# The last expert step's second layer in two column halves, each with a bank and a store of its own

## The chip, the core and the metric

The kernel runs on one core of one Trainium2 chip. The metric is device time in microseconds of one execution. Five engines run side by side, each with its own instruction stream: PE (TensorE, matrix products; its weight loads are listed as PEld), ACT (ScalarE), DVE (VectorE), POOL (GpSimd) and SP (SyncE, which here issues the loads). They wait for each other by semaphores. PE writes into PSUM banks, from which ACT or DVE carries results to SBUF. Data go to and from HBM by DMA; the stores of this kernel's result are indirect DMAs (each row to its own place) that POOL issues.

## The reference

The first part is attention with random features over 8 batches, 8 heads and 576 positions; its result, 4608 rows (tokens) of 512, is the input `x` of a mixture of 8 experts, of which each row takes one:

```python
logits = xn @ en.T / tau
expert_idx = np.argmax(logits, axis=1)
...
gate_w = probs[np.arange(N), expert_idx]
out = np.zeros((N, D), dtype=np.float32)
for e in range(E):
    mask = expert_idx == e
    ...
    h = np.maximum(x[mask] @ w1[e], 0.0)
    out[mask] = gate_w[mask, None] * (h @ w2[e])
```

N is 4608, D (`DM` in the kernel) 512, E 8, and the hidden width F 1024.

## The kernel before

The attention part writes its rows, sorted by expert, into a table `xs` in HBM. With a row stand its router logits and, in its last element, the token's number, that is, the row of the output it belongs to. The expert part then goes through **steps** of 128 rows that all belong to one expert. Which expert and which rows a step has is only known at run time and stands in a small table `tabi`, from which the engines read registers. Steps 0 to 37 (`NSTAT` is 38) are written out in the program; `ends` is 37, the last of them. A loop at the end of the program takes further steps if the table has more; how many steps there are is copied to `nsteps` (L1318), every engine reads it (L1321), and branches (L1322). In the profiled execution the loop isn't entered.

A step's work: the first layer (rows times `w1`, the products in tiles named `pb` in the trace), the transposition of the hidden rows, and the second layer (`down`, hidden rows times `w2`, into a PSUM tile `po`). Operands are float32 split in a high and a low part (`hh`, `hl` for the hidden rows; `w2h`, `w2l` for the weights), and each product is the sum of three matmuls: high with high, high with low, low with high. `products` (L275 on) writes them out: for the second layer 8 blocks of the hidden width times 3, so 24 matmuls with 512 columns each. Since the buffer half that holds a step's weights is a register's value, the weights' address is made by a register instruction of PE's sequencer before each of these matmuls (`ISA` in the listings of order, `FUSED_REGOPS` in the trace).

`finished(v)` takes the second layer's result: it is scaled by the rows' gates into a tile `xgp` (two buffers, taken in turn), and the returned function calls `store` (L314), an indirect DMA from POOL that writes 128 rows of 512 floats to the places that the tokens' numbers in `tail` name. For the last step, `finished(ends, True)` scales columns 0 to 255 on ACT (L1158) and columns 256 to 511 on DVE (L1159), both from the one bank. One store follows, and then the copy of the step count.

The order on every engine is the order in which the program is written (`manual_schedule`). Two places matter here. Before the last step's scaling POOL has an explicit `nc.gpsimd.drain()` (L1316), behind the store of step 36. And the end of the program, behind the loop, has all engines meet; SP waits there for the semaphores of all DMAs, the stores' among them.

The end of the expert part before, L1309 to L1318:

```python
inverted(totals[batch(ends)[0]])
split("w2", ends - 1)
finished(ends - 2)()
down(ends, both)
finished(ends - 1)()
split("w2", ends)
nc.gpsimd.drain()
finished(ends, True)()
nc.gpsimd.tensor_copy(nsteps, tabi[:, 0:1])
```

Of the kernel before, what the change touches and what calls it, by code (L numbers as in the profile page):

```python
# [13 lines left out]
I32 = mybir.dt.int32  # L14
BF16 = mybir.dt.bfloat16
U16 = mybir.dt.uint16
AF = mybir.ActivationFunctionType
ALU = mybir.AluOpType
# [4 lines left out]
P = 128  # L23
B, H, S, D, M = 8, 8, 576, 64, 128
E, F = 8, 1024
N = B * S
DM = H * D
# [12 lines left out]
NPRE = 2  # L40
# [24 lines left out]
def attention_moe(ctx: ExitStack, tc: tile.TileContext, qT, kT, v1, omT, emb, tau, w1q, w2q, xs, out):  # L65
    nc = tc.nc
# [10 lines left out]
    nu = [nuu[:, a] for a in range(2)]  # L77
# [47 lines left out]
    xgp = [const.tile([P, PAY], F32, name=f"xgp{t}") for t in range(NPRE + 1)]  # L125
# [43 lines left out]
    def reg(kind, t):  # L169
        i, eng, mx = kinds[kind]  # L170
        g = t // 16
        if (kind, g) not in regs:
            n = min(16, NSTAT - g * 16)
            regs[kind, g] = nc.values_load_multi_w_load_instructions(
                tabi[i : i + 1, g * 16 : g * 16 + n], engines=[eng], min_val=0, max_val=mx,
                skip_runtime_bounds_check_because=WHY,
            )[1]
        return regs[kind, g][t % 16]
# [36 lines left out]
    def computed(wn, t, ms):  # L215
        for m in ms:
            seq[m] = len(seq)
        for o in range(NSTAT):
            apart(wn, spl.get((wn, o), ()), o, ms, t)
        if t >= NQ and (wn, t) not in mmi:  # L220
            for w in spl[wn, t - 1]:
                tc.add_manual_dep(ms[0].ins, w.ins.name, sync, reason="the weights")
        mmi.setdefault((wn, t), []).extend(ms)
# [48 lines left out]
        else:  # L272
            low()

    def products(dst, a, wn, par, cs, half, begin, end):  # L275
        ah, al = a
        _, wh, wl = W[wn]
        done = []
        for i, c in enumerate(cs):
            for k, (x, w) in enumerate(((ah, wh), (ah, wl), (al, wh))):  # L280
                if wn == "w1":
                    ws = w[:, ds(par, 1), c, half * 512 : (half + 1) * 512]
                else:
                    ws = w[:, ds(par, 1), c // 2, (c % 2) * 512 : (c % 2 + 1) * 512]
                done.append(nc.tensor.matmul(  # L285
                    dst, x[:, c * P : (c + 1) * P], ws.rearrange("p o f -> p (o f)"),
                    start=(begin and i == 0 and k == 0), stop=(end and i == len(cs) - 1 and k == 2),
                ))
        return done

    def scaled(po, xg, gate):
        nc.vector.tensor_scalar(xg[:, 0:DM], po, gate, None, op0=ALU.mult)
# [18 lines left out]
    def few(name, t, n):  # L311
        return gp.tile([P, n], F32, name=f"{name}{t}", tag=name, bufs=2)

    def store(t, xg, tail=None):  # L314
        w = nc.gpsimd.indirect_dma_start(  # L315
            out=out, out_offset=bass.IndirectOffsetOnAxis(ap=(xg[:, DM:] if tail is None else tail)[:, E : E + 1].bitcast(I32), axis=0),
            in_=xg[:, 0:DM], in_offset=None, bounds_check=N - 1, oob_is_err=False,
        )
        for o in outs:
            tc.declare_no_dep(w.ins, o.ins.name, reason="other tokens")  # L320
        outs.append(w)

    with ExitStack() as c1:
        p1 = c1.enter_context(tc.tile_pool(name="p1", bufs=2))
# [415 lines left out]
        early, spare, mid, ends, behind = {}, {}, {}, {}, []  # L740
        uses = iter(range(NTILE * 4))
        ring = lambda: next(uses) % 3
        at = lambda d, *key: d.setdefault(key, [])
# [16 lines left out]
        for i in range(NTILE + LAG + 2):  # L760
# [177 lines left out]
            if i in LOADS:  # L938
                n = LOADS[i]
# [16 lines left out]
        t = lambda n, w=E, dt=F32: once.tile([P, w], dt, name=n)  # L956
# [24 lines left out]
        cs, nt = cs_nt[:, 0, :], cs_nt[:, 1, :]  # L981
# [30 lines left out]
        both = once.tile([P, 3, E], F32, name="both")  # L1012
# [33 lines left out]
    p2 = ctx.enter_context(tc.tile_pool(name="p2", bufs=2))  # L1046
# [6 lines left out]
    def bank(name, tag, bufs=1):  # L1053
        return shared(tag) if bufs == 2 else ps.tile([P, 512], F32, name=name, tag=tag)
# [33 lines left out]
    xg, xt, hid, raws, po = {}, {}, {}, {}, {}  # L1088
# [31 lines left out]
    with tc.manual_schedule(engines={ET.PE, ET.Activation, ET.DVE, ET.Pool, ET.SP}):  # L1120
        xt[NPRE] = pre_x[0]
        turn, ends = {}, NSTAT - 1
# [28 lines left out]

        n2s, rough, nrms, totals, gates, tails = {}, {}, {}, {}, {}, {}

        def finished(v, halves=False):
            y = xgp[v % NPRE]
            if halves:
                p, m = po.pop(v), DM // 2
                nc.scalar.activation(y[:, 0:m], p[:, 0:m], AF.Copy, scale=gates[v])  # L1158
                nc.vector.tensor_scalar(y[:, m:DM], p[:, m:DM], gates[v], None, op0=ALU.mult)  # L1159
            else:  # L1160
                scaled(po.pop(v), y, gates[v])
            return lambda: store(v, y, tails[v])
        batch = lambda t: divmod(t - NPRE, 3)

# [29 lines left out]
        def down(u, cs):  # L1194
            if cs[0] == 0:
                po[u] = bank(f"po{u}", f"kv{u % 2}")
            par = reg("par", u) if u >= NQ else 0
            computed("w2", u, products(po[u], hid[u], "w2", par, cs, 0, cs[0] == 0, cs[-1] == 7))
# [5 lines left out]
        low, high, both = range(4), range(4, 8), range(8)  # L1204
        for t in range(NPRE, NSTAT):
# [11 lines left out]
            if early:  # L1217
                wn = joined(t - 1)
# [91 lines left out]
        inverted(totals[batch(ends)[0]])  # L1310
        split("w2", ends - 1)
        finished(ends - 2)()
        down(ends, both)
        finished(ends - 1)()
        split("w2", ends)
        nc.gpsimd.drain()  # L1316
        finished(ends, True)()
        nc.gpsimd.tensor_copy(nsteps, tabi[:, 0:1])  # L1318


    tot = nc.values_load(nsteps[4:5, 0:1], min_val=0, max_val=NSTEP, skip_runtime_bounds_check_because=WHY)  # L1321
# [70 lines left out]
```

## Time and profile before

| | us |
|---|---|
| median of 3 timed runs | 632.24 (632.17 to 633.24) |
| the profiled execution's own time | 632.94 |
| its span, first to last instruction of the program | 631.3 |
| PE busy | 620.7 (98%) |
| POOL busy | 421.7 (67%) |

The span is 1.6 us shorter than that execution's time; what lies around it is not in the trace. The granted clock of PE is 0.999 of full speed over the span. PE is busy nearly throughout, but its last matmul ends at about 625.4, and the last 5.9 us of the span belong to what comes behind it: scaling, store, the step count, and the meeting of the engines at the end. The rows for that stretch stand in the section behind the next one. In the profile "busy" leaves out register, branch and semaphore instructions; their groups are found by asking for a source line.

### The profile page before, as it was taken

To read this page: it belongs to the slowest core of one execution; us is meant where nothing else is said; L and a number is where in the kernel's file an instruction comes from. 1 tells how busy PE (TensorE), PEld (TensorE's weight loads), DVE (VectorE), ACT (ScalarE), POOL (GpSimd) and SP (SyncE) were. 2 spreads that over 40 slices of the span, in tenths; PEclk is the share of its full clock that TensorE was granted. 3 is DMA by queue.
4 is the path that set the end of the run, shared out by engine and by line. 5 is a ranking of instruction groups with operands and counts; after the bars stand their busy time and mean duration, and the time that the engine had idled before them with its cause. 6 is when DMAs were issued, how large, how long until landed. Compare 5 with 4: busy or idle time off the path is not lost.

```text
span 631.3 us, 19167 instructions
## 1 busy us (share of the span) xinstructions
PE 620.7 (98%) x6337; PEld 531.3 (84%) x6338; DVE 493.2 (78%) x916; ACT 432.9 (69%) x1136; POOL 421.7 (67%) x603
## 2 busy tenths in 40 slices
PE   9999999999999999999999999999999999999996
PEld 8999999998978788888888888888888888888884
DVE  5799899898889836779787877778687886878754
ACT  6999899899997327676756666656666656675640
POOL 3013344356787544588897878787887989797952
PEclk9999999999999999999999999999999999999999
DMA  7655776777772488698887796968687786878541
GB/s 258 217 153 168 225 200 210 220 221 251 245 256 87 153 271 265 199 258 231 246 204 245 177 263 189 229 203 229 208 212 239 202 247 175 246 202 236 172 117 46
DMA packets 143262, 132.18 MB, mean 209 GB/s; under 512 B 107766, under 2 KB 107894, under 8 KB 143168
## 3 DMA queue, kind: packets, MB, share of 16 engines
q1 hardware_dynamic: 136544, 109.96, 61.3%
q0 software_dynamic: 6480, 20.91, 8.6%
q8 instruction: 57, 0.93, 0.6%
q14 instruction: 37, 0.30, 0.2%
q10 hardware_dynamic: 144, 0.07, 0.0%
HBM read 83.78 MB, written 21.97 MB: 168 GB/s over the span
## 4 chain that ended last, share of the span: by engine, by line
PE 70%; DVE 3%; ACT 2%; issue 0%; POOL 0%; ACTq 0%; DVEq 0%
PE pb L285 31%; PE po L285 31%; PE fs_o L285 2%; PE pb L374 1%; PE nuu L483 1%; ACT ftq L388 1%; PE pb L267 1%; PE fs_a L285 1%; DVE nmq L378 1%; PE kva L406 1%; PE pb L463 0%; DVE qp L470 0%; DVE xr L508 0%; ACT qp L468 0%; ACT sq L296 0%
## 5 line engine op out<-in xcount | busy, mean ns | idle before, releaser
L240 POOL TENSOR_TENSOR w2l<-raww,w2h 128x256 f32 x128 | 142.8, 1116 | 7.6
L240 POOL TENSOR_TENSOR w1l<-raww,w1h 128x256 f32 (+1 forms) x130 | 114.0, 877 | 14.5 <-DVE w1h L234 6.0
L285 PE MATMUL po<-w2h,hh 128*128 (+1 forms) x288 | 112.2, 390 | 0.0
L285 PE MATMUL po<-w2h,hl 128*128 (+1 forms) x288 | 112.1, 389 | 0.0
L285 PE MATMUL po<-w2l,hh 128*128 (+1 forms) x288 | 112.0, 389 | 0.0
L285 PE MATMUL pb<-w1h,xh 128*128 (+1 forms) x280 | 109.3, 390 | 0.0
L285 PE MATMUL pb<-w1h,xl 128*128 (+1 forms) x280 | 109.0, 389 | 0.0
L285 PE MATMUL pb<-w1l,xh 128*128 (+1 forms) x280 | 108.9, 389 | 0.0
L1110 DVE COPY pl<-pb 128x512 uint16<-128x512 uint16 x68 | 46.8, 690 | 59.9 <-ACT pl L1106 59.3
L1106 ACT ACTIVATE pl<-pb 128x512 uint16<-128x512 uint16 x68 | 39.5, 584 | 71.8 <-PE pb L285 69.4
L388 ACT ACTIVATE ftq<-pb,nmq 128x128 f32<-128x128 f32 x288 | 80.0, 413 | 3.6 <-DVE nmq L378 3.6
L315 POOL DMA_INDIRECT y<-xgp,tail x36 | 44.8, 1246 | 53.8 <-DVE w1h L234 27.8
L388 ACT ACTIVATE ftk<-pb,nmk 128x128 f32<-128x128 f32 x272 | 75.9, 470 | 4.9 <-DVE nmk L378 4.9
L1128 DVE COPY wd<-t 128x1024 uint16<-128x1024 uint16 x68 | 64.2, 945 | 1.5 <-DMA t<-pl 1.5
L1144 ACT ACTIVATE hh<-wd 128x1024 fp32r<-128x1024 f32 x34 | 36.2, 1063 | 41.3 <-DVE wd L1128 36.7
L285 PEld LDWEIGHTS po<-w2h,hh 128*128 128x128 f32 x288 | 54.1, 188 | 11.2
L285 PEld LDWEIGHTS po<-w2l,hh 128*128 128x128 f32 x288 | 54.1, 188 | 11.2
L285 PEld LDWEIGHTS po<-w2h,hl 128*128 128x128 f32 x288 | 54.0, 187 | 11.2
L285 PEld LDWEIGHTS pb<-w1h,xl 128*128 128x128 f32 x280 | 52.6, 188 | 10.9
L285 PEld LDWEIGHTS pb<-w1l,xh 128*128 128x128 f32 x280 | 52.6, 188 | 11.0
L285 PEld LDWEIGHTS pb<-w1h,xh 128*128 128x128 f32 x280 | 52.5, 187 | 10.7
L582 POOL DMA_INDIRECT xs<-xr,posi x36 | 36.4, 1011 | 36.8 <-PE nuu L463 26.4
(346 smaller groups left out, 1265.7 us busy)
## 6 DMA issues: line engine op xcount, KB each, us to landing
raww<-w1q SPq DMA_DIRECT2D x38, 512.0 KB, 4.0
raww<-w2q SPq DMA_DIRECT2D x38, 512.0 KB, 5.2
qt<-qT SPq DMA_DIRECT2D x36, 256.0 KB, 3.7
kt<-kT SPq DMA_DIRECT2D x35, 256.0 KB, 3.4
xg<-xs SPq DMA_DIRECT2D x23, 260.5 KB, 3.0
xgp<-xs SPq DMA_DIRECT2D x15, 260.5 KB, 4.9
rf<-w1q SPq DMA_DIRECT2D x4, 512.0 KB
rf<-w2q SPq DMA_DIRECT2D x4, 512.0 KB, 5.8
```

The source lines that it names most:

```text
L240: ils.append(eng.tensor_tensor(at(l, d)[:, c], raw[:, c], at(h, d)[:, c].bitcast(F32), op=ALU.subtract))
L267: nc.tensor.transpose(bank[:, c * P : (c + 1) * P], src[:, o + c * P : o + (c + 1) * P], ident)
L285: done.append(nc.tensor.matmul(dst, x[:, c * P : (c + 1) * P], ws.rearrange("p o f -> p (o f)"), start=(begin and i == 0 and k == 0), stop ...
L315: w = nc.gpsimd.indirect_dma_start(out=out, out_offset=bass.IndirectOffsetOnAxis(ap=(xg[:, DM:] if tail is None else tail)[:, E : E + 1].b ...
L374: nc.tensor.matmul(st["pj" + w, i, a][:, c, :], st[w, i][r, c, :], om[r, :], start=True, stop=True)
L378: nc.vector.tensor_reduce(nm, st["pj" + which, i, a], axis=AX.X, op=ALU.max, negate=True)
L388: nc.scalar.activation(ft[:, h, :], pj[:, h, :], AF.Exp, bias=nm[:, h : h + 1])
L582: w = nc.gpsimd.indirect_dma_start(out=xs, out_offset=bass.IndirectOffsetOnAxis(ap=posi[:, j : j + 1], axis=0), in_=xr, in_offset=None, bo ...
L1106: nc.scalar.activation(planes[1][:, o : o + 512], halved(src)[:, :, 1], AF.Copy)
L1110: nc.vector.tensor_copy(planes[0][:, o : o + 512], halved(src)[:, :, 0])
L1128: nc.vector.tensor_copy(to, src)
L1144: nc.scalar.activation(hh, wd[:, 0:F], AF.Relu)
```

## The change

The second layer of step 37 is no longer one group of 24 matmuls with 512 columns. It is two groups of 24 matmuls with 256 columns: the first writes columns 0 to 255 into the bank `po`, the second writes columns 256 to 511 into another bank (`nu[1]`, free at that time). ACT scales the first half as soon as the first group is done, and a store of its own writes it; DVE scales the second half from the other bank, and a second store writes that. For the stores the output is seen as 9216 rows of 256 floats, and the places are twice the token's number plus 0 or 1; two small DVE instructions compute them into a new tile `places`. The copy of the step count stands between the two stores.

```diff
-    def products(dst, a, wn, par, cs, half, begin, end):
+    def products(dst, a, wn, par, cs, half, begin, end, cols=slice(0, DM)):
...
-                    ws = w[:, ds(par, 1), c // 2, (c % 2) * 512 : (c % 2 + 1) * 512]
+                    ws = w[:, ds(par, 1), c // 2, (c % 2) * 512 + cols.start : (c % 2) * 512 + cols.stop]
...
-    def store(t, xg, tail=None):
+    def store(t, xg, tail=None, to=None):
+        if to is None:
+            to, at, n, cols = out, (xg[:, DM:] if tail is None else tail)[:, E : E + 1].bitcast(I32), N, slice(0, DM)
+        else:
+            to, at, n, cols = out.rearrange("n (a d) -> (n a) d", a=2), *to
         w = nc.gpsimd.indirect_dma_start(
-            out=out, out_offset=bass.IndirectOffsetOnAxis(ap=(xg[:, DM:] if tail is None else tail)[:, E : E + 1].bitcast(I32), axis=0),
-            in_=xg[:, 0:DM], in_offset=None, bounds_check=N - 1, oob_is_err=False,
+            out=to, out_offset=bass.IndirectOffsetOnAxis(ap=at, axis=0),
+            in_=xg[:, cols], in_offset=None, bounds_check=n - 1, oob_is_err=False,
         )
...
-        down(ends, both)
+        y, m, par = xgp[ends % NPRE], DM // 2, reg("par", ends)
+        places = p2.tile([P, 2], I32, name="places", bufs=1)
+        for a in range(2):
+            nc.vector.tensor_scalar(places[:, a : a + 1], tails[ends][:, E : E + 1].bitcast(I32), 2.0, float(a), op0=ALU.mult, op1=ALU.add)
+        parts = [(bank(f"po{ends}", f"kv{ends % 2}")[:, 0:m], slice(0, m)), (nu[1][:, 0:m], slice(m, DM))]
+        for p, cols in parts:
+            computed("w2", ends, products(p, hid[ends], "w2", par, both, 0, True, True, cols))
         finished(ends - 1)()
         split("w2", ends)
         nc.gpsimd.drain()
-        finished(ends, True)()
+        (p0, c0), (p1, c1) = parts
+        nc.scalar.activation(y[:, c0], p0, AF.Copy, scale=gates[ends])
+        store(ends, y, to=(places[:, 0:1], 2 * N, c0))
         nc.gpsimd.tensor_copy(nsteps, tabi[:, 0:1])
+        nc.vector.tensor_scalar(y[:, c1], p1, gates[ends], None, op0=ALU.mult)
+        store(ends, y, to=(places[:, 1:2], 2 * N, c1))
```

The old `halves` form of `finished` goes with it. What this does to the order is seen best on two engines. (`DMA` is an indirect store; `y` is the output, `xgp` the scaled rows, `tail` the token numbers.)

POOL at the end of the program, before; the rows between the two pieces belong to the loop, which isn't entered (the branch goes from the first L1322 row to the second):

```order
L240 TENSOR_TENSOR w1l<-raww_37_9042,w1h 128x1024 [waits DMAHW5_49,DVE_49]
L315 DMA y<-xgp_140,tail_8833 4608x512 [waits DMASW6_49,DVE_49,Activation_49]
L315 DMA y<-xgp_139,tail_8942 4608x512 [waits DMASW7_49,DVE_49,Activation_49]
L315 DMA y<-xgp_140,tail_9040 4608x512 [waits DMASW0_49,DVE_49]
L1318 COPY nsteps<-tabi 5x1
L1321 TENSOR_LOAD nsteps [waits Pool_49]
L1322 COMPARE_AND_BRANCH
...
L1322 ISA [waits Pool_49,Pool_sequencer_49,DMASW1_49]
L1322 UNCONDITIONAL_BRANCH
L1388 ISA [waits barrier_Pool_Activation_PE_DVE_SP_gather]
```

POOL at the same place, after:

```order
L240 TENSOR_TENSOR w1l<-raww_37_9042,w1h 128x1024 [waits DMAHW5_49,DVE_49]
L319 DMA y<-xgp_140,tail_8833 4608x512 [waits DMASW6_49,DVE_49,Activation_49]
L319 DMA y<-xgp_139,tail_8942 4608x512 [waits DMASW7_49,DVE_49,Activation_49]
L319 DMA y<-xgp_140,places 9216x256 [waits DMASW0_49,Activation_49]
L1325 COPY nsteps<-tabi 5x1
L1330 TENSOR_LOAD nsteps [waits Pool_49]
L1331 COMPARE_AND_BRANCH
...
L1331 ISA [waits Pool_49,Pool_sequencer_49,DMASW1_49]
L1331 UNCONDITIONAL_BRANCH
L319 DMA y<-xgp_140,places 9216x256 [waits DMASW2_49,DVE_49]
L1397 UNCONDITIONAL_BRANCH
```

The second store stands not only behind the copy of the step count but behind the read of it and the branch. The drain (L1316 before) stands in both ahead of the third `DMA`; this listing leaves drains out.

DVE at the end of the program, before (`po_9192`, `po_9233` and `po_9266` are the second layers of steps 35, 36 and 37):

```order
L292 TENSOR_SCALAR xgp_140<-po_9192,totalb_9145 128x512 [waits DMASW4_49]
L292 TENSOR_SCALAR xgp_139<-po_9233,totalb_9145 128x512 [waits DMASW5_49,PE_49]
L234 ISA
L234 COPY w2h<-raww_37_9217 128x1024 [waits DMAHW2_49]
L240 ISA
L240 TENSOR_TENSOR w2l<-raww_37_9217,w2h 128x1024 [waits DVE_49]
L1159 TENSOR_SCALAR xgp_140<-po_9266,totalb_9145 128x256 [waits DMASW6_49,Activation_49]
```

DVE at the same place, after:

```order
L292 TENSOR_SCALAR xgp_140<-po_9192,totalb_9145 128x512 [waits DMASW4_49]
L1315 TENSOR_SCALAR places<-tail_9040 128x1 x2
L292 TENSOR_SCALAR xgp_139<-po_9233,totalb_9145 128x512 [waits DMASW5_49,PE_49]
L234 ISA
L234 COPY w2h<-raww_37_9217 128x1024 [waits DMAHW2_49]
L240 ISA
L240 TENSOR_TENSOR w2l<-raww_37_9217,w2h 128x1024 [waits DVE_49]
L1326 TENSOR_SCALAR xgp_140<-nuu,totalb_9145 128x256 [waits DMASW6_49,PE_49]
```

The two instructions for `places` come in ahead of step 36's scaling, and the last scaling waits for PE where it waited for ACT.

## Rows read from the trace of the kernel before

**Rows 1.** The page's head, and the tail of the chain that ended last (start us, us, what).

```profile
span 631.3 us, 19167 instructions
PE 620.7 (98%) x6337; PEld 531.3 (84%) x6338; DVE 493.2 (78%) x916; ACT 432.9 (69%) x1136; POOL 421.7 (67%) x603
...
614.47 10.91 PE po L285 x48
625.38 0.03 ACTq L1158
625.40 0.05 issue
625.45 0.48 ACT xgp L1158
625.93 0.03 issue
625.96 0.49 DVE xgp L1159
626.45 0.27 issue
626.72 0.98 POOL y L315
627.70 0.16 POOL nsteps L1318
```

**Rows 2.** What SP's queue waited for, 620 to 632 us (total us, times, longest).

```profile
SPq L1321 <- POOL nsteps L1318: 16.6, 1, 16.6
SPq L1388 <- DMA y<-xgp,tail: 0.2, 1, 0.2
```

**Rows 3.** POOL's timeline to the end (start us, us, instruction [idle before <- releaser]).

```profile
619.75 0.99 POOL L315 DMA_INDIRECT y<-xgp,tail  x1 [6.46 <-DVE xgp L292]
621.50 1.92 POOL L315 DMA_INDIRECT y<-xgp,tail  x1 [0.76 <-issue]
626.72 0.98 POOL L315 DMA_INDIRECT y<-xgp,tail  x1 [3.30 <-DVE xgp L1159]
627.68 0.18 POOL L1318 COPY nsteps<-tabi 5x1 int32<-5x1 int32 x1
```

**Rows 4.** Lines L1316, and L315 at 616 to 628 us (ns min/median/max, first and last start).

```profile
L1316 POOLq DRAIN  x1: 3875/3875/3875, 621.3 to 621.3; - x1
...
L315 POOLq MOVE  x3: 29/29/29, 616.8 to 625.2; - x3
L315 POOLq EVENT_SEMAPHORE  x3: 17/1158/2094, 616.9 to 625.3; - x3
...
DMA to landing us min/median/max: 2.7/2.7/3.5
```

**Rows 5.** Lines L1322 and L1388, POOL's sequencer at the branch and the program's end.

```profile
L1322 POOLq INC_SWDGE_SEM  x1: 203/203/203, 628.7 to 628.7; - x1
...
L1388 POOLq DRAIN  x3: 109/193/585, 628.9 to 630.9; - x3
```

**Rows 6.** DVE's timeline at 615.5 to 632 us.

```profile
615.90 0.16 DVE L308 TENSOR_SCALAR totalb<-totalb 128x3 f32<-128x3 f32 x1
...
618.22 0.74 DVE L292 TENSOR_SCALAR xgp<-po,totalb 128x512 f32<-128x512 f32 x1
619.96 0.75 DVE L292 TENSOR_SCALAR xgp<-po,totalb 128x512 f32<-128x512 f32 x1 [0.99 <-PE po L285]
...
625.96 0.48 DVE L1159 TENSOR_SCALAR xgp<-po,totalb 128x256 f32<-128x256 f32 x1 [3.39 <-ACT xgp L1158]
```

**Rows 7.** PE's timeline: transposes, and step 37's first and last second-layer matmuls.

```profile
613.43 1.03 PE L267 MATMUL pb<-ident,wd 128*128 128x128 f32 x8
...
619.76 0.39 PE L285 MATMUL po<-w2h,hh 128*128 x1
619.99 0.39 PE L285 MATMUL po<-w2l,hh 128*128 x1
...
624.98 0.39 PE L285 MATMUL po<-w2h,hl 128*128 x1
```

**Rows 8.** Line L285 from 618.5 us on, PE's sequencer and weight loads.

```profile
L285 PEldq FUSED_REGOPS  x23: 46/55/60, 619.1 to 622.1; - x23
...
L285 PEld LDWEIGHTS po<-w2l,hh x10: 187/188/188, 618.4 to 624.5; 128*128 128x128 f32 x10
```

**Rows 9.** DMA from 626 to 632 us in 40 slices: busy tenths, rate, and the store's landing.

```profile
DMA  0000000000000009998300620000000000000100
GB/s 0 0 0 0 0 0 0 0 0 0 0 0 0 0 0 410 382 410 314 137 0 0 164 55 0 0 0 0 0 0 0 0 0 0 0 0 0 55 0 0
...
y<-xgp,tail POOLq DMA_INDIRECT x1, 2.7
```

More of the change, by code (lines that the diff above doesn't have):

```diff
@@ L1152, in attention_moe, with finished @@
         n2s, rough, nrms, totals, gates, tails = {}, {}, {}, {}, {}, {}
-        def finished(v, halves=False):
+        def finished(v):
             y = xgp[v % NPRE]
[L1156 to L1161, printed above, removed]
+            scaled(po.pop(v), y, gates[v])
             return lambda: store(v, y, tails[v])
```

## The prediction

> **What bounds the kernel now.** I read the chain of waits from its end. PE leads it until the last matmul ends at 625.38, and the change touches nothing ahead of step 37, so the question is what follows: ACT's half of the scaling, then DVE's half behind it, POOL's store at 626.72, the copy of the step count [rows 1]. The chain as printed ends with the copy, but the span goes on to 631.3, and the copy isn't what it waits for. SP's waits tell what is: at the end of the program SP waited 0.2 us for the landing of the last store [rows 2], that is, SP had come round from the copy and the branch and still found the store in flight. The store takes 2.7 us from issue to landing [rows 9], so it lands at 626.72 + 2.67 = 629.4, and 1.9 us more go by until the span ends. So the end is set by **the start of the last store**, and the copy comes only some 0.2 us behind it. This is the quantity to follow: in the kernel before it is 626.72.
>
> Two things hold a store back: its data and POOL. Before, it was the data: DVE ended at 625.96 + 0.48 = 626.44 and the store started 0.28 later [rows 6, 3]. POOL was ready, but not by much. Its drain (L1316) began at 621.3 and took 3.9 us, so it ended at about 625.15; it had to sit out the store of step 36, which started at 621.50, took 1.92 [rows 3] and lands 3.5 after its start, at 625.0 (it is the largest of the three landings there) [rows 4]. POOL's last register and semaphore instructions of L315 come right behind, at 625.2 and 625.3 [rows 4]. Before, this left POOL 1.1 us of slack against 626.44. The drain is in no chain of waits, since it waits in the shadow of PE.
>
> **The change part by part.** *The first half on ACT, and its store.* The first 24 matmuls end at about half of step 37, near 623, and ACT's scaling takes 0.48 [rows 1], so the data are ready before 624. But the store stands behind the same drain, and nothing that the drain waits for moves: step 36's scaling and store stay where they were. So the first store can't be issued before 625.3. How long is it from there? Three stores show two prices. The last one stood ready and started 0.28 after its data [rows 3, 6]. The stores at 619.75 and 621.50 had to be let through by a separate semaphore instruction ahead of them; they started 0.79 after DVE's ends at 618.96 and 620.71 [rows 6, 3], with the instruction's own idle time of 0.76 put down to issue. The first half's store is of the second kind (its semaphores have long been there when the drain ends, and dispatch begins then), so I take 0.75 after the semaphore instruction at 625.3: start 626.05, with 0.28 as the other bound. It is busy 0.98, as the last one was [rows 3].
>
> *The copy, its read and the branch between the stores.* By the listing of POOL's order, what stands between the stores is not the copy alone but also the read of the count and the branch of the not-entered loop. Before, the copy started 0.96 after its store's start [rows 3], and from the copy's start to the drain at the program's end it was 628.9 - 627.68 = 1.2 us, with the last instruction of the branch at 628.7 [rows 3, 5]. So after: copy at 627.0, branch done at 628.2. This stretch is covered by nothing, since POOL does it itself, between two stores.
>
> *The second store.* Its register and semaphore instructions cost 0.1 us (625.2 and 625.3 in rows 4), and dispatch 0.75 again: it starts at about **629.05**, against 626.72. Its data are there long before: see next. That is **+2.33 us** on the quantity that sets the end.
>
> *The second half on DVE.* DVE no longer waits for ACT, which takes the 0.51 us between the two halves' starts off the data's path [rows 1]. But the data's path isn't the late one any more, so it is worth nothing here.
>
> *The matmuls.* 48 with 256 columns in place of 24 with 512. Before, one starts every 0.227 us (619.76 to 624.98 in 23 steps) [rows 7]. No row shows 256 columns in this form. From below, half of that is 0.113: no cost. The nearest row is the sequencer's: it makes an address for each matmul, and between 619.1 and 622.1 it issued 23 of them, one in 0.136 us [rows 8], while PE lagged behind; with twice as many matmuls half as long this becomes the pace. 48 x 0.136 = 6.5 from 619.13, so the last matmul starts near 625.5 and ends near 625.9, 0.5 later than before; DVE is done at 626.45. The store's data are then 2.6 us early, and this cost is hidden. From above: the shown 0.188 of a weight load [rows 8] can't be the pace, since transposes with loads go by at 0.109 each ((1.03 - 0.27)/7, with 0.27 for the last one's own length) [rows 7]; if a load lay wholly bare beside each matmul, 0.109 + 0.113 = 0.222. POOL needs the data by 628.75, which holds up to a pace of 0.17 us. TensorE: Matmul & The Clock Gate of the Trainium skill, section "LDWEIGHTS (loading the stationary operand)", gives a load of 128 columns as 107 ns; by it a pair would be 107 + 109 = 216 ns if bare, a result like that upper end, and hidden if the load runs under 256 columns as it does here under 512.
>
> *Two small DVE instructions.* 0.16 each, as the small one at 615.90; they fall where DVE waits 0.99 us for PE ahead of step 36's scaling [rows 6]. Cost nothing; without that cover 0.3 us on step 36's store, and so on the drain.
>
> *The landing.* Half the bytes. The transfer itself shows as 0.8 us of busy DMA slices (some 5.5 of 0.15 us) out of the 2.67 [rows 9]; halved, it is 0.4 less: 2.3. The bounds are 2.27 and 2.67 (the upper one if half the bytes take as long); I take 2.32, **-0.35 us**. DMA: Bandwidth & Descriptors of the Trainium skill, section "Anatomy of one DMA — SWDGE (gpsimd) path", fits 2.0 us plus bytes at 436 GB/s, which is 2.6 for this store and would be 2.3 for half of it; it also has the fixed part constant, whatever the size.
>
> *After the landing.* The same 1.9 us: the engines' meeting. SP and the others now come to it early, since the count is copied 0.7 us earlier, and wait.
>
> *The sum.* +2.33 - 0.35 = **+2.0 us**. Against the profiled execution's own time of 632.94 this is 634.9; that execution is 0.7 above the median of the timed runs, 632.24, so for the median I say **634.2**. With the bounds (dispatch 0.28 twice: -0.9; landing 2.67: +0.35; dispatch 0.79: +0.1) this case goes from 633.3 to 634.7. A difference of 0.2%, 1.26 us, is about what a measurement can tell here.
>
> **The rivals.**
>
> *The drain lets the first store go early, and the kernel is not slower.* If the drain's length in the trace was mere idling, and it could end with step 36's store at 623.42 rather than with its landing, the first store would start near 624.3, the copy at 625.2, and the branch would be done at 626.4, all under PE's last matmuls. The second store, let through at 626.5, would start between 626.7 and 627.25, land 2.3 later, at 629.0 to 629.6, and the span would move by -0.4 to +0.2: about 632.1. It decides from a first store ahead of about 624.5. Against it: in the row the drain does end at 625.15, right where step 36's store lands, and no wait of it is taken away. For it: one execution shows one such drain. Chance 0.13.
>
> *Both stores are dispatched at the short price.* 0.28 instead of 0.75 twice, with a short landing: +1.0, 633.2, within what can be told. For it: the last store before. Against it: the two ahead of it. Chance 0.09.
>
> *The matmuls become the bound.* Weight loads bare at a pace of 0.222: PE ends at 619.76 + 48 x 0.222 + 0.1 = 630.5, DVE at 631.1, the second store starts at 631.3 and lands at 633.6: +4.2, 636.4. Against it: no pair in the trace shows a bare load, the transposes' 0.109 least of all. Chance 0.04.
>
> **How the numbers follow.** The forecast (POOL's serial chain behind the drain) has 0.74. The predicted time is its own, 634.2. Slower by over 0.2%: 0.74 plus 0.04 plus a little of the short dispatch, 0.80. Within 0.2%: most of the short dispatch and of the early drain, 0.17. Faster: 0.03, the early drain with everything at its lower end. The range of 633.0 to 635.2 holds the forecast's bounds, a little more above for the code behind the branch, which hasn't run in the trace at that place, and the short dispatch; it leaves out the early drain and the slow matmuls.
>
> **What would show it.** In the profile after: the drain ending near 625.15, the first store starting near 626 although ACT ended near 623.4; the copy near 627; the second store near 629.05, with idle time ahead of it that is put to POOL's own issue and not to DVE; DVE's half done near 626.5; SP waiting some 3 us for the last landing, near 631.4; 256-column matmuls 0.12 to 0.14 us apart. A first store ahead of 624.5, or a second one that starts right behind DVE, would prove the forecast wrong.

## The result and the profile after

The changed kernel takes **636.34 us** (median of 6 runs, 635.49 to 637.13) against 632.30 for the kernel before (6 runs): a ratio of 1.0054, interval 1.0043 to 1.0066, that is 2.7 to 4.2 us more. It is slower, as forecast, but by more than the 2.0 us forecast, and the time lies above the range of 633.0 to 635.2. The profiled execution took 636.18, its span 634.6 against 631.3.

All times below are us from the start of the span. Programs that are the same up to the last steps come to step 35's store at different times (between 619.4 and 625.1 in the runs of this document), so where kernels are compared I count from the start of that store, the first of the three or four that end the program: "at +6.97" is 6.97 us behind it. For the kernel before it is 619.75 [rows 3], its last store starts at +6.97 and its span ends at +11.5. For the changed kernel it is 620.16, the last store starts at +10.08 and the span ends at +14.4. The 2.9 us of this difference lie inside the interval of the timed runs (2.7 to 4.2), near its lower end, while the medians differ by 4.0. The 0.41 by which step 35's store itself is later in this one execution, and what else of the 4.0 the 2.9 doesn't cover, are not explained here.

POOL's row of instructions at the end of the changed kernel (timeline; columns: start, duration, engine, line, operation, and in brackets the idle time before it and what ended it). It answers to [rows 3]:

```profile
620.16 0.98 POOL L319 DMA_INDIRECT y<-xgp,tail  x1 [6.44 <-DVE places L1315]
621.91 1.92 POOL L319 DMA_INDIRECT y<-xgp,tail  x1 [0.77 <-issue]
627.19 0.97 POOL L319 DMA_INDIRECT y<-xgp,places  x1 [3.36 <-issue]
628.15 0.18 POOL L1325 COPY nsteps<-tabi 5x1 int32<-5x1 int32 x1
630.24 0.97 POOL L319 DMA_INDIRECT y<-xgp,places  x1 [1.91 <-DVEq L1331]
```

Lines 1 and 2 are the stores of steps 35 and 36, lines 3 and 5 the two halves of step 37. The idle time of 3.36 ahead of the first half ends with "issue": no engine was waited for. The bracket of line 5 names another engine's sequencer at the branch; DVE had the scaled half ready at 627.05, over 3 us before. The timeline of DVE and of ACT shows that the data were early:

```profile
619.30 0.20 DVE L1315 TENSOR_SCALAR places<-tail 128x1 int32<-128x1 int32 x2
620.38 0.75 DVE L292 TENSOR_SCALAR xgp<-po,totalb 128x512 f32<-128x512 f32 x1 [0.87 <-PE po L285]
...
626.57 0.48 DVE L1326 TENSOR_SCALAR xgp<-nuu,totalb 128x256 f32<-128x256 f32 x1 [3.58 <-PE nuu L285]
```

```profile
623.30 0.47 ACT L1323 ACTIVATE xgp<-po,totalb 128x256 f32<-128x256 f32 x1 [7.73 <-PE po L285]
```

The first half was scaled at 623.77 and its store started at 627.19; the second was scaled at 627.05 and its store started at 630.24. What lay between is POOL's drain, by the view of its line (operation, count, duration in ns, first and last start), which answers to the first line of [rows 4]:

```profile
L1321 POOLq DRAIN  x1: 4649/4649/4649, 621.7 to 621.7; - x1
```

4.65 us in place of 3.88: it ended at 626.33, not at 625.15. And SP at the end of the program, in answer to the 0.2 us of [rows 2]:

```profile
SPq L1397 <- DMA y<-xgp,places: 3.1, 1, 3.1
```

Why the drain was longer is seen in the DMA view, here for the 5 us in which step 36's store is under way (40 slices, of 0.115 us here and 0.125 in the second view; first row the busy share of 16 DMA engines in tenths, second row GB/s; at the end the store's time from issue to landing). The kernel before, 621.4 to 626.0:

```profile
DMA  9799800000000000000000679760000000000000
...
q0 software_dynamic: 147, 0.39, 21.8%
...
y<-xgp,tail POOLq DMA_INDIRECT x1, 3.5
```

The changed kernel, 621.8 to 626.8:

```profile
DMA  9899500000000000600028965300000000000000
GB/s 393 328 426 393 197 0 0 0 0 0 0 0 0 0 0 0 131 0 0 0 98 344 426 262 230 66 0 0 0 33 0 0 0 0 0 0 0 0 0 0
...
q0 software_dynamic: 149, 0.40, 20.9%
q8 instruction: 1, 0.02, 1.5%
...
y<-xgp,tail POOLq DMA_INDIRECT x1, 4.3
```

The first block of digits is step 35's store, the second step 36's. Between them stands something that the kernel before doesn't have: one packet on queue q8, kind "instruction". Its slice shows 131 GB/s, which over 0.125 us is 16 KB, and a busy share of 0.6 of 16 engines, which is 1.2 us: one packet of 16 KB that occupied one DMA engine for 1.2 us, from 623.85 on, just as step 36's packets were about to come. Behind the store's block a straggler of 33 GB/s follows, one packet of 4 KB. In the trace's list of packets it is the second of two late ones of this store: they start at 625.05 and 625.54, and the instruction packet ends at 625.06. The store landed 4.3 us after its issue in place of 3.5. Its semaphore is updated 16 times, once for each part of the store; by these landing events, 15 of the parts were there at 625.45 and the last at 626.22; the drain ended 0.12 later, at 626.33. In the kernel before the two were 625.02 and 625.03, and the drain ended 0.12 later.

So the reading is: **POOL's serial chain behind the drain, as forecast, and a fetch of instructions that held the drain itself up.** PE's program has 24 more pairs of weight load and matmul, each with an address instruction, so PE comes further in its program before it is done. In the kernel before, the last fetch on q8 came at 604.76, and the next at 629.4, together with two smaller ones on q14 at the branch, just as the last store had landed. The experiments take this apart.

### The profile page after: what moved, and what is told of

Its sections match the earlier page's. It is cut to its first block, busy times and chain, and to the rows that moved or that the text cites. A ratio compares the mean times of both kernels' runs of the same rounds, so it can differ in the third digit from the quotient of the medians.

```text
span 634.6 us, 19244 instructions
## 1 busy us (share of the span) xinstructions
PE 621.9 (98%) x6361; PEld 533.4 (84%) x6362; DVE 495.7 (78%) x918; ACT 433.1 (68%) x1136; POOL 420.8 (66%) x604
## 5 line engine op out<-in xcount | busy, mean ns | idle before, releaser
L285 PE MATMUL po<-w2h,hh 128*128 (+1 forms) x288 | 111.4, 387 | 0.0
L285 PE MATMUL po<-w2h,hl 128*128 (+1 forms) x288 | 111.2, 386 | 0.0
L285 PE MATMUL po<-w2l,hh 128*128 (+1 forms) x288 | 111.2, 386 | 0.0
L285 PE MATMUL pb<-w1h,xh 128*128 (+1 forms) x280 | 109.4, 391 | 0.0
L285 PE MATMUL pb<-w1h,xl 128*128 (+1 forms) x280 | 109.1, 390 | 0.0
L285 PE MATMUL pb<-w1l,xh 128*128 (+1 forms) x280 | 109.0, 389 | 0.0
L1132 DVE COPY wd<-t 128x1024 uint16<-128x1024 uint16 x68 | 65.5, 965 | 1.6 <-DMA t<-pl 1.5
L285 PEld LDWEIGHTS po<-w2h,hl 128*128 128x128 f32 x288 | 54.1, 188 | 10.9
L285 PEld LDWEIGHTS po<-w2h,hh 128*128 128x128 f32 x288 | 54.1, 188 | 10.9
L285 PEld LDWEIGHTS po<-w2l,hh 128*128 128x128 f32 x288 | 54.0, 188 | 10.9
L285 PEld LDWEIGHTS pb<-w1h,xh 128*128 128x128 f32 x280 | 52.5, 188 | 11.0 <-issue 0.2
L285 PEld LDWEIGHTS pb<-w1h,xl 128*128 128x128 f32 x280 | 52.5, 188 | 11.0 <-DVE xl L269 0.2
L285 PEld LDWEIGHTS pb<-w1l,xh 128*128 128x128 f32 x280 | 52.7, 188 | 10.9
```

The costliest lines, as they stand in the source:

```text
L285: done.append(nc.tensor.matmul(dst, x[:, c * P : (c + 1) * P], ws.rearrange("p o f -> p (o f)"), start=(begin and i == 0 and k == 0), stop ...
L1132: nc.vector.tensor_copy(to, src)
```

## The experiments

Theory T1: the end is POOL's chain of drain, store, copy, read, branch, store; the drain lasts until step 36's store has landed. Theory F, formed on the trace above: the drain got longer since PE's next fetch of instructions now falls into that store's flight. The rivals were that the stores or their landings cost the time themselves (R1), that stores queue behind each other when no drain separates them (R2), and that the doubled matmuls or the other code at the end cause it without a fetch (R3, M).

**The drain alone, out of the changed kernel.**

```diff
         split("w2", ends)
-        nc.gpsimd.drain()
```

> The changed kernel without the drain ahead of its first store; all else as it is. Theory T1 (the end is POOL's serial chain behind the drain, and the drain waits until step 36's store has landed): the first store starts 0.3 to 0.8 after step 36's store is issued, near 624.5, the copy, its read and the branch go by under PE's last matmuls, and the second store starts 0.3 to 0.75 behind DVE's half (627.05), at 627.3 to 627.8 in place of 630.24. Landing 2.4, so the time falls by 2.4 to 2.9 us, to about 633.6. Rival R1 (the loss is in the two stores or their landings themselves, whatever lets them go): the time stays at 635.5 or more. Rival R2 (without the drain, the store queues behind step 36's store and takes its 1.9 in place of 1.0, each time): first store near 624.5 but long, second store 628 or later, 634.5.

Measured: ratio to the kernel before 1.0003 (interval 0.9988 to 1.0018), so the loss can no longer be told from nothing. POOL's timeline:

```profile
623.60 1.92 POOL L319 DMA_INDIRECT y<-xgp,tail  x1 [0.77 <-issue]
625.82 0.97 POOL L319 DMA_INDIRECT y<-xgp,places  x1 [0.30 <-ACT xgp L1322]
626.79 0.18 POOL L1324 COPY nsteps<-tabi 5x1 int32<-5x1 int32 x1
628.96 0.97 POOL L319 DMA_INDIRECT y<-xgp,places  x1 [1.99 <-DVE xgp L1325]
```

The first half's store starts 0.30 behind the end of step 36's, with ACT's half done at 625.46; the second starts 0.29 behind DVE's half, at +7.11. T1 holds, R1 and R2 fall. The span ended at +12.3, later than the 11.5 to 12.0 expected: the second store took 3.1 us to land in place of 2.4, since 15 of its parts were there at 631.35 and the last at 632.09. The branch is taken ahead of this store, and a 16 KB packet follows the branch (629.78).

**The copy behind both stores, drain kept.**

```diff
-        nc.gpsimd.tensor_copy(nsteps, tabi[:, 0:1])
         nc.vector.tensor_scalar(y[:, c1], p1, gates[ends], None, op0=ALU.mult)
         store(ends, y, to=(places[:, 1:2], 2 * N, c1))
+        nc.gpsimd.tensor_copy(nsteps, tabi[:, 0:1])
```

> The changed kernel with the copy of the step count behind the second store, as it stands behind the last store in the kernel before; so its read and the branch are out of the way between the stores. The drain stays. T1: first store unmoved at about 0.85 behind the drain's end; the second store no longer waits for copy, read and branch (1.2 us) and the semaphore instruction behind them; it starts 0.1 to 0.75 after the first one's 0.97, that is 1.3 to 2.0 us earlier than now. Now the copy and the branch come behind the second store, under its flight of 2.4. Time down by 1.3 to 2.0, to 634.3 to 635.0. Rival R1 (the loss is in the stores and landings, not in what stands between them): 636.3, no change.

Measured: ratio 1.0013 (0.9987 to 1.0038). The two stores stand together:

```profile
632.43 0.97 POOL L319 DMA_INDIRECT y<-xgp,places  x1 [3.68 <-issue]
633.70 0.98 POOL L319 DMA_INDIRECT y<-xgp,places  x1 [0.30 <-issue]
```

1.27 us from start to start in place of 3.05: copy, read, branch and the second dispatch cost 1.78 us in the changed kernel. The last store is at +8.63. It could have been earlier still, but the drain took 4.97 here; the q8 packet was there again, at +4.02.

**The drain alone, out of the kernel before.**

```diff
         split("w2", ends)
-        nc.gpsimd.drain()
         finished(ends, True)()
```

> The kernel before without the drain ahead of its last store: the drain's price by itself. T1: that store waited for its data (DVE's end) by 1.1 us, so without the drain its start stays 0.28 behind DVE and the time stays at 632.3, within 0.3. Rival R2 (a store that follows another one in flight takes 1.9 in place of 1.0 us, or starts later): the last store is busy 1.9 and lands later, 633.0 to 633.5. A gain of over 0.5 would say that the drain was on the path already, against T1.

Measured: ratio 1.0001 (0.9983 to 1.0020); last store again at +6.97, busy 0.98. Where the data are late, the drain costs nothing, and its absence wins nothing.

**The halves in two banks alone, with one store.**

```diff
-        store(ends, y, to=(places[:, 0:1], 2 * N, c0))
-        nc.gpsimd.tensor_copy(nsteps, tabi[:, 0:1])
         nc.vector.tensor_scalar(y[:, c1], p1, gates[ends], None, op0=ALU.mult)
-        store(ends, y, to=(places[:, 1:2], 2 * N, c1))
+        store(ends, y, tails[ends])
+        nc.gpsimd.tensor_copy(nsteps, tabi[:, 0:1])
```

> The matmul part of the change alone: second layer of step 37 in two halves of columns with a bank each, ACT scales the first as soon as it is there and DVE the second, then one store of both, and the copy behind it as in the kernel before. The drain stays ahead of the store. T1 with the drain tied to the landing of step 36's store: PE ends 0.2 to 0.6 later than in the kernel before, DVE doesn't wait for ACT, so the data are ready between 626.1 and 626.6 on the clock of the kernel before. If the drain ends at 625.15 as there, the store starts at 626.2 to 626.7 and the time is 631.8 to 632.3. If the instruction fetch comes with the doubled matmuls and holds up step 36's store here too, the drain takes about 4.6 and ends near 625.9, the store starts near 626.7, 632.3. Rival R3 (the changed kernel's extra time came from the doubled matmuls and the code around them): over 633.5.

Measured: ratio 1.0013 (0.9996 to 1.0031), too wide to tell it from no change; the trace tells more. DVE's half was done at +6.83, 0.14 behind the kernel before, but the store started at +8.06, where 6.45 to 6.95 were expected, or 6.95 with the fetch (626.2 to 626.7 on the clock of the kernel before), and the span ended at +12.6, 1.1 later than before. The drain took 5.65 us, and the same view as above (622.6 to 628.6, slices of 0.15 us) shows the packet:

```profile
L1321 POOLq DRAIN  x1: 5649/5649/5649, 622.5 to 622.5; - x1
```

```profile
GB/s 355 410 355 246 0 0 0 0 0 0 0 0 0 0 0 0 0 382 396 219 219 0 109 0 0 0 0 0 0 0 0 0 0 0 0 0 0 0 0 0
...
q8 instruction: 1, 0.02, 1.1%
```

The lone 109 GB/s is 16 KB in 0.15 us. 15 parts of step 36's store were there at 626.21, the last at 627.99, and the drain ended at 628.10. So the doubled matmuls alone, with the single store kept, bring the fetch and a drain that comes behind the data. The expectation of 4.6 for this case was too low, and so was its time of no loss, but it named the right cause. By the medians alone (1.1 us above the kernel before, where R3 had over 1.2) R3 is not far off; it is the trace that shows the fetch and the drain behind it.

**PE's program shifted, the kernel before.**

```diff
-WARM = 28
+WARM = 52
```

> The kernel before with one number changed: 52 warm-up matmuls at the program's start in place of 28. Nothing is touched near the end; the 24 more (each a weight load and a matmul, 48 instructions, read by nothing) only move PE's later instructions on by as many places in its program. Theory F (PE's instructions are fetched in packets of 16 KB, one per some 85 matmuls, the 24 more matmuls of the change let PE reach the next fetch while step 36's store is in flight, and the fetch holds one DMA engine's part of the store up): the fetch that here came at 629.4, behind the end, moves to within about 2 us of PE's last matmul, that is, 3 to 6 us behind the start of step 35's store; if it meets the store's packets, the last of the 16 parts lands 0.7 to 1.8 us behind the others and the drain takes 4.6 to 5.7 in place of 3.88. Rival M (it is the doubled matmuls or the other code at the end that delay the landing): no such fetch, drain 3.8 to 3.9. The start costs some 2.5 us in either case.

Measured, one run of 634.9 with the longer start: a packet on q8 came at +2.45, and none came at the branch, where the kernel before has its own at +9.65. Nothing but PE's program was changed, so the packet is PE's. But it came ahead of the 3 to 6 us expected, between the two stores' packets, and met none; the drain took 3.88 and the last store started at +6.97. It doesn't tell F from M. So did a second try:

```diff
-WARM = 28
+WARM = 40
```

> The kernel before with 40 warm-up matmuls at the start in place of 28 (the run with 52 put the fetch at 2.45 us behind the start of step 35's store, between the two stores' packets, where it met none). 12 fewer of them put PE's instructions 24 places back, which is 8 matmuls of three instructions or 1.8 us at 0.227: the fetch at about 4.2 us behind the start of step 35's store, as in the changed kernel and its variants (3.7 to 5.0). Theory F: it meets step 36's store there, one of the 16 parts lands 0.7 to 1.8 us behind the rest, and the drain takes 4.6 to 5.7 in place of 3.88, in a kernel whose end is that of the kernel before in every instruction; the last store starts at 6.97 to 8.0 behind step 35's. Rival M (the doubled matmuls or the new code at the end delay the landing): drain 3.88, last store at 6.97.

One run of 635.37; the fetch came at +2.84, not at 4.2, and touched the store only just: the last part landed 0.12 behind the rest, the drain took 4.00, the last store was at +6.97. With unsplit matmuls PE's sequencer is through with its address instructions early (its last is at 622.1, +2.4, in [rows 8]), which may be why the fetch can't be moved later than that; this is argued, not shown.

**PE's program shifted, the changed kernel.**

```diff
-WARM = 28
+WARM = 58
```

> The changed kernel with 58 warm-up matmuls at the start in place of 28, all else untouched: PE's later instructions stand 60 places further on. Theory F: the fetch comes some 2.5 to 3 us earlier, ahead of step 36's store, 0.8 to 2.3 us behind the start of step 35's store; the store then lands whole and the drain takes 3.9 in place of 4.65, and the last store starts 9.2 to 9.4 us behind the start of step 35's store in place of 10.1. Rival M: drain 4.6 or more, last store at 10.1 again. The start costs some 3 us in either case, so the time itself tells little; the stretch from step 35's store to the end tells it: 13.6 against 14.4.

This one decides. The instructions of the end are those of the changed kernel, all of them, and only their place in PE's program is another:

```profile
L1321 POOLq DRAIN  x1: 3882/3882/3882, 624.3 to 624.3; - x1
```

```profile
627.71 0.47 ACT L1323 ACTIVATE xgp<-po,totalb 128x256 f32<-128x256 f32 x1 [9.56 <-DMA y<-xgp,tail]
```

The fetch came at +2.43, step 36's store landed whole (its last part 0.02 behind the rest), and the drain was back at 3.88. The expectation had the fetch at 0.8 to 2.3, a little earlier. The last store started at +9.31 and the span ended at +13.7, as F had it (9.2 to 9.4, 13.6). M falls: all the code that it blames is there. The time itself was 637.95 (4 runs, ratio 1.0099, interval 1.0063 to 1.0136), with 30 more matmuls at the start. The second row shows where the fetch went instead: it held one part of step 35's store 2.1 us behind the others (625.46 and 627.60), and ACT's first half, which writes the tile that this store reads, waited for it until 627.71. In the kernel before with 24 more at the start a packet at the same place held nothing up; what decides between the two isn't shown.

**The two stores alone, one bank, matmuls unsplit.**

```diff
-        parts = [(bank(f"po{ends}", f"kv{ends % 2}")[:, 0:m], slice(0, m)), (nu[1][:, 0:m], slice(m, DM))]
-        for p, cols in parts:
-            computed("w2", ends, products(p, hid[ends], "w2", par, both, 0, True, True, cols))
+        whole = bank(f"po{ends}", f"kv{ends % 2}")
+        parts = [(whole[:, 0:m], slice(0, m)), (whole[:, m:DM], slice(m, DM))]
+        computed("w2", ends, products(whole, hid[ends], "w2", par, both, 0, True, True))
```

> The stores' part of the change alone: the second layer of step 37 in 24 matmuls of 512 columns and one bank as in the kernel before, then ACT's half, its store, the copy, DVE's half, its store. Theory F with T1: no fetch before PE's end, so the drain is 3.9, ending 5.4 behind the start of step 35's store. The first store waits for ACT now (done at 6.2) and starts at 6.45 to 6.9; copy, read, branch and the semaphore instruction again 2.2 to 3.05 behind it, second store at 9.5 to 9.95, the end 13.8 to 14.3 behind step 35's store (14.44 in the changed kernel, 11.5 in the kernel before). Rival M: as long a drain as in the changed kernel though no matmul is split.

Measured: ratio 1.0031 (1.0020 to 1.0042). No fetch ahead of the end, drain 3.88, as F expects. The first store started at +6.45, as expected. My expectation of the second one, 9.5 to 9.95, was wrong: its register and semaphore instructions come at 625.6 here, ahead of the copy and not behind the branch, and so it started 0.34 behind the copy, at +7.74. Yet the span ended at +13.5, only 0.3 ahead of the 13.8 expected. The DMA view of its flight (627.0 to 631.5):

```profile
q8 instruction: 1, 0.02, 1.9%
q14 instruction: 2, 0.02, 1.6%
...
y<-xgp,places POOLq DMA_INDIRECT x1, 3.9
```

3.9 us to landing, where the second store of the changed kernel took 2.4: 15 parts at 630.08, the last at 631.01. Three packets of instructions that come with the branch, one of 16 KB and two of 8 (628.40 to 628.55), met this store. Of the 2.0 us by which the span ends later than before, 0.77 is the later start and about 1.2 the longer flight (3.90 against the 2.67 of the whole store before).

**Drain away, copy behind both stores.**

```diff
-        nc.gpsimd.drain()
         (p0, c0), (p1, c1) = parts
         nc.scalar.activation(y[:, c0], p0, AF.Copy, scale=gates[ends])
         store(ends, y, to=(places[:, 0:1], 2 * N, c0))
-        nc.gpsimd.tensor_copy(nsteps, tabi[:, 0:1])
         nc.vector.tensor_scalar(y[:, c1], p1, gates[ends], None, op0=ALU.mult)
         store(ends, y, to=(places[:, 1:2], 2 * N, c1))
+        nc.gpsimd.tensor_copy(nsteps, tabi[:, 0:1])
```

> The changed kernel without the drain and with the copy of the step count behind both stores: what is left of the change when its two costs on POOL are gone. T1: first store 4.0 behind the start of step 35's store, as without the drain alone; the second one 0.28 behind DVE's half, at about 7.1 (6.97 for the last store of the kernel before, 10.1 in the changed kernel). Half the bytes land in 2.4 in place of 2.67, so the end is at 11.4 to 11.6 if no fetch meets it, and 12.2 if one does as it did without the drain. Time within 0.1% of the kernel before: the halves bring no gain, since the doubled matmuls run at the sequencer's pace and end 0.4 to 0.5 later, which is what ACT's wait cost. Rival: a gain of over 1 us, if the early first half is worth what its earlier data suggest.

Measured: ratio 0.9999 (0.9990 to 1.0008). Second store at +7.17, landing 2.4 later, end at +11.6, as expected for a last store that no fetch meets. The fetch hit step 36's store here too:

```profile
y<-xgp,tail POOLq DMA_INDIRECT x1, 4.9
```

It landed 4.9 us after its issue, its last part 1.4 behind the rest, and the first half's store behind it took 3.0 in place of 2.4; nobody waited for either. With both costs on POOL gone, no gain or loss of the halves can be told.

**The kernel before, scaling in one piece.**

```diff
-        finished(ends, True)()
+        finished(ends)()
```

> The kernel before with step 37's scaling as one piece of 512 columns on DVE in place of two halves, ACT's and then DVE's. The rows show 0.75 for one such piece and 0.47 + 0.04 + 0.48 for the two that follow each other. If what matters is the start of the last store, it comes 0.25 us earlier, 6.7 behind step 35's store in place of 6.97, and the end likewise (about 11.3): 0.04% of the time, less than the runs can tell. Rival: the one piece starts later behind PE's end than ACT's half did, and nothing is won.

Measured: ratio 0.9996 (0.9979 to 1.0014). The piece took 0.75 as expected and was done at +6.41, earlier than the 6.69 of the two halves, but the store started at +7.18, not 6.7. In the kernel before, the wait for DVE stood in the store itself, which started 0.28 behind it. Here it stands in the separate semaphore instruction, which ended at 626.65, and the store started at 627.38, 0.73 later. The half microsecond of dispatch ate the gain, for a reason that neither side of the expectation had.

**All kernels in one table** (times from the start of step 35's store; "late" is the last of the 16 parts of step 36's store behind the fifteenth, by the landing events; "fetch" the start of the first 16 KB packet on q8 behind step 35's store, which in the rows with 9 us and more is the one at the branch; values from rounded times, good to 0.01; for "changed, no drain" the trace has 13 of the 16 landing events):

| kernel | fetch | late | drain | last store | span ends |
|---|---|---|---|---|---|
| before | 9.65 | 0.01 | 3.88 | 6.97 | 11.5 |
| changed | 3.69 | 0.77 | 4.65 | 10.08 | 14.4 |
| changed, no drain | 4.73 | 1.65 | none | 7.11 | 12.3 |
| changed, copy last | 4.02 | 1.09 | 4.97 | 8.63 | 13.0 |
| before, no drain | 9.69 | 0.01 | none | 6.97 | 11.4 |
| two banks, one store | 4.99 | 1.77 | 5.65 | 8.06 | 12.6 |
| before, 24 more at the start | 2.45 | 0.01 | 3.88 | 6.97 | 11.5 |
| before, 12 more at the start | 2.84 | 0.12 | 4.00 | 6.97 | 11.5 |
| changed, 30 more at the start | 2.43 | 0.02 | 3.88 | 9.31 | 13.7 |
| one bank, two stores | 9.13 | 0.01 | 3.88 | 7.74 | 13.5 |
| changed, no drain, copy last | 3.96 | 1.39 | none | 7.17 | 11.6 |
| before, one piece | 9.87 | 0.01 | 3.88 | 7.18 | 11.7 |

Five kernels have the fetch between 3.7 and 5.0, and their step 36's store is late by 0.8 to 1.8; in the seven others it is late by 0.12 at most. In these five the last part lands 1.03 to 1.16 us behind the end of the fetch's packet, whenever that is, which ties the one to the other. In all nine with a drain, the drain ended 0.12 behind the last landing.

A count of PE's instructions in the traces bears theory F out over all twelve kernels. In the eight with a fetch ahead of the branch, PE had begun 14528 to 14579 instructions when the packet started. The four without one, the kernel before among them, have begun 14525 with the last matmul of the second layer; the changed kernel comes to 14597 there. What is left open: the five kernels have the same number of PE instructions, yet the fetch came anywhere from 3.69 to 4.99, and its cost to the landing went from 0.8 to 1.8 with it. The 0.77 of the changed kernel is one execution's.

## Why the prediction was right about the kind and wrong about the size

- **What sets the end** (the start of the last store): right. 10.08 - 6.97 = 3.11 later, and the end of the span 2.9 later.
- **The chain on POOL behind the drain**: right to a tenth. From the drain's end to the last store I had 629.05 - 625.15 = 3.90; measured 630.24 - 626.33 = 3.91. In pieces: the semaphore instruction to the first store 0.75 (0.75 assumed), store 0.97 (0.98), copy to the end of the branch 1.2 (1.2), the second dispatch 0.8 (0.75). Taking it away (copy last) and making it unnecessary (no drain) showed it each time.
- **The drain's end: the step that failed.** "But the store stands behind the same drain, and nothing that the drain waits for moves". Step 36's scaling and store did stay where they were, but the store's landing did not, because the longer PE program brought PE's next fetch of instructions into its flight. The drain took 0.77 more (4.65 in place of 3.88). I had weighed the 24 additional pairs by their pace alone, and of the traffic near the end I had counted only the kernel's own transfers. The rows for it were in the trace of before: late in the program a packet of 16 KB comes on q8 every 17 to 21 us, one per some 85 matmuls, the last at 604.76, with the next one due at just about PE's last matmul.
- **The sum**: +2.0 forecast; on the tail 2.9 measured, which is +2.1 on the chain (2.33 - 0.26 with the landing as measured) and +0.77 for the drain. The range had put a few tenths above the forecast's bounds for code behind the branch, and nothing for the drain's end. These 0.77 alone would bring the forecast of 634.2 to about 635.0, still under 635.2. The medians differ by 4.0, and the 1.1 beyond the tail's 2.9 are not explained: 0.4 lay ahead of step 35's store in the two profiled executions, and a longer drain in other executions, as the four variants show it, is possible but not shown.
- **The landing**: 2.41 (630.24 to 632.65) for half the bytes, where I took 2.32 between 2.27 and 2.67. DMA: Bandwidth & Descriptors of the Trainium skill, section "Anatomy of one DMA — SWDGE (gpsimd) path", fits 2.0 us plus bytes at 436 GB/s, by which an estimate is 2.3; the trace has 0.1 more for this store. From the landing to the end it was 1.9 again, as assumed.
- **The matmuls**: hidden, as forecast. The 24 of the first half start 0.120 apart, the 24 of the second (623.05 to 626.24) 0.139 apart, near the 0.136 of the sequencer, whose last address instruction is at 626.0. Counted from step 35's store, the second layer ended 0.7 later than before where I had 0.5, and DVE's half was done at 627.05, 3.2 us ahead of its store. The rival of bare weight loads at 0.222 is out.
- **Two small DVE instructions**: 0.20 together by the row in place of 0.16 each, and beside the wait for PE.
- **The rival of the early drain** is out: with nine drains ending 0.12 behind the last landing, at lengths from 3.88 to 5.65, it isn't mere idling. **The rival of short dispatch** is out for this kernel, since both stores came 0.75 to 0.8 behind their semaphore instruction. But the price depends on the program: 0.28 to 0.30 where the store's own instruction waits or its wait was settled early (copy last, no drain), 0.73 to 0.8 behind a separate semaphore instruction that just went through.
- **Would the halves have won anything without POOL's two costs?** None that the runs can tell: 0.9999 (0.9990 to 1.0008), and the span ends at +11.6 in place of +11.5. ACT's early half takes 0.5 us off the data's path, and the doubled matmuls give it back, since they end 0.7 later (6.4 in place of 5.6 behind step 35's store).

## What to carry to other kernels

When a change adds instructions to an engine near the end of a program, look at where that engine's instruction fetches fall and which transfers they will meet, not only at the engine's own time: here 72 more PE instructions cost 0.7 us on PE, which nothing waited for, and 0.8 us on a store that a drain waits for. A drain ahead of a store is free as long as the store's data are later than the drain; a change that makes the data early pays the drain in full, so take the two together. And whatever ends in a branch goes behind the last store, not between two.

## What the runs showed of the hardware that I had not expected

- A packet of 16 KB of instructions takes 0.9 to 1.6 us on its DMA engine, and a store whose packets it met landed with one of its 16 parts 0.7 to 2.1 us behind the other fifteen. Runtime: NRT & Kernel Launch of the Trainium skill, section "Instruction fetch mechanics", has fetches in blocks of 16 KiB, 256 instructions, and calls crossing such a boundary mostly hidden. The size and the spacing agree (85 matmuls of three instructions are 255); here the changed kernel's PE was done 3.2 us ahead of what its data were needed for, crossing included, but the store that the fetch met was not spared.
- A branch brings such packets as well (628.40 to 628.55 in the kernel with one bank), and a store in flight behind it took 3.1 us (changed kernel without the drain) and 3.9 us (one bank) to land in place of 2.4. In the changed kernel itself the packets at the branch were through at 631.43, the second store's began at 631.8, and it landed in 2.4.
- POOL's drain behind an indirect store ended 0.12 us after the last part had landed, in nine of nine runs, 3.88 to 5.65 us long.
- The last store of the kernel before started 0.28 us after its data when it waited for them itself; with a semaphore instruction ahead of it waiting (scaling in one piece) it started 0.73 behind that instruction, 0.77 after its data.
